# A fused attention and gated-MLP kernel on one core: an input load, a reduction and a bound are moved in the first passes

## The chip, the core and the metric

The kernel runs on one core of a Trainium2 chip. A core has five engines that run their own instruction streams beside each other and meet only at semaphores: TensorE (PE in the profile; PEld is its weight load), VectorE (DVE), ScalarE (ACT), GpSimd (POOL) and SyncE (SP, which here only issues DMAs). The metric is device time of one execution in microseconds (us); lower is better. The kernel before took 1939.83 us, the median of three runs (1937.18, 1939.83 and 1940.55).

## The reference, cut to what matters

```
xn = layernorm(x)                                   # x: 2048 x 640
q  = xn @ wq                                        # 32 heads of 192
p  = softmax(q @ k_cache.T * 192**-0.5)             # 2048 queries x 2048 keys, per head
s  = (p @ v_cache) @ wo
g  = silu((silu(xn @ w1) * (xn @ w3)) @ w2)         # F = 1536
out = x + s * g
```

All tensors are bf16. Softmax doesn't need the exact maximum of a row: any shift that is no smaller than the scores, and not so large that the sums vanish, gives the same result.

## The kernel before, in words

**Tiling.** The 2048 queries are 16 tiles of 128 rows (x tiles 0 to 15), taken in four blocks of 512 (`qb` 0 to 3). A head's pass over one block has eight steps `p` 0 to 7. In a step TensorE makes the scores of two key tiles for the 512 queries (`scores`, six 64-row matmuls on line 505 into one of two PSUM tiles `st2`), ScalarE takes the exponential (`weights`, line 512, with the shift `nb` as bias) and TensorE multiplies by the values (`values`, line 545, 16 matmuls, into the two PSUM tiles `ob0` and `ob1`). At the end of a pass `evict` (line 521) reduces each of the two on VectorE; the next pass can't write `ob0` or `ob1` before its reduction is done. `values` returns pieces that are put in a list, and `advance` takes them from it some steps late, so that TensorE has work while ScalarE makes the exponentials.

**The bound.** The shift `nb` isn't the row maximum but an upper bound of the block: for each of the 192 dimensions the largest absolute query times the largest absolute key, summed. `query_max` (line 376) and `key_maxima` (line 414) make the maxima on VectorE and keep them in the tile `st`; `bound` (lines 442 to 448) multiplies them, sums two columns into `ns`, and lets GpSimd sum over the 128 partitions (`partition_all_reduce`, line 448). For the first two heads only part of the data is looked at, and `compare_bounds` later computes the full bound and keeps the difference in `gaps`; if that were over 32, or a sum vanished, an exact path would be run. `next_bound(h, qb)` is the bound of head `h` for one block.

**The first passes.** They go in the order of `order`: (head 0, block 0), (head 1, block 0), (0, 1), (0, 2), (0, 3), (1, 1), (1, 2), (1, 3). So the pass of head 1 over block 0 is the second and the pass of head 0 over block 1 is the third. Into these passes the layer norm of the x tiles is woven by hand: `extras` and `posts` name what follows step `p` of pass `n`, as `(n, p)`. A tile's layer norm is `ln_stats` (two `bn_stats` and a `bn_aggr` on VectorE, lines 237 and 238), `ln_root` (logarithm and exponential on ScalarE, lines 244 and 247), `ln_scale` (VectorE, line 255) and `dma_turn` (a transposing DMA issued by SyncE, line 266, into `xnT`). Around the change:

- `(0, 0)`: `complete_second`, GpSimd's copies of head 1's keys into `KC` (lines 154 and 155, columns 0 to 511 and then 512 to 1023 of a half) and a memset of ones
- `(0, 2)`: scale and turn x tiles 4 and 5, and the first key maxima of head 1
- `(0, 4)`: `next_bound(1, 0)`, the shift of the second pass
- `(0, 5)`: `ln_stats` of x tiles 6 and 7
- `(1, 0)`, `(1, 1)`: `ln_root(6)`; scale and turn tiles 6 and 7
- `(1, 5)`: `ln_root(8, 4)` and `late_project(0, 1)`, head 0's queries of block 1 (line 348). Its first part has ten matmuls on x tiles 4 and 5 and then ten on 6 and 7; the casts, the maxima, `next_bound(0, 1)` and a copy of rows into `qD` (`lower_rows`, line 388) follow in `second`.

In the passes `n` = 3 to 6 a list `looked[h]` of further maxima is worked off on VectorE, one or two per step; it ends with `compare_bounds(h)`.

**The order of the transfers.** Nearly all loads of the start are on SyncE's queue, in program order: keys of head 1 (`KB`, line 124), the first part of head 1's values (`load_values_part`, line 143, two DMAs), then x tiles 6 and 7 (`load_x`, line 194), x tiles 8 and 9, the second part of head 1's values, x tiles 10 and 11; then the transposes of x tiles 4 to 7. `pin` keeps the program order of an engine for what it wraps; everything that the change touches is pinned.

After the first passes come the heads 2 to 31 (a whole head takes about 51 us), the rest of the MLP, and the output projection.

Of the kernel before, what the change touches and what calls it, by code (L numbers as in the profile page):

```python
# [30 lines left out]
def _kernel_impl(ctx, tc, A_x, A_k_cache, A_v_cache, A_wq, A_wo, B_w1, B_w3, B_w2, out):  # L31
    nc = tc.nc
# [33 lines left out]
    pin = tc.keep_in_program_order  # L66
# [35 lines left out]
    def load_weights(h, eng, keep):  # L102
        w = wqp.tile([P, DC, 2 * P], BF16, tag="w")
        wsel = B_w1 if h % 2 == 0 else B_w3
        m = h // 2

        def load(c0, c1, src, s0):
            return lambda eng: keep(eng.dma_start(out=w[:, :, c0:c1],  # L108
                                                  in_=src[:, s0:s0 + c1 - c0].rearrange("(c p) d -> p c d", p=P)))

        if h < 2:
            steps = [load(0, DH, A_wq, h * DH), load(DH, 2 * P, wsel, m * PGW)]
        else:
            steps = [load(0, P, A_wq, h * DH), load(P, P + PGW, wsel, m * PGW), load(P + PGW, 2 * P, A_wq, h * DH + P)]
        ws = (w[:, :, 0:P], w[:, :, P:2 * P])
        if eng is None:
            return ws, steps
        for step in steps:
            step(eng)
        return ws  # L120

    def load_key_part(h, s, half, k0, k1, keep):
        d0 = (0, DH - P)[s]
        return keep(nc.sync.dma_start_transpose(out=half[:, k0:k1], in_=A_k_cache[0, h][k0:k1, d0:d0 + P]))  # L124

    def load_key_half(h, s, keep):
        half = kvp.tile([P, SK], BF16, tag=("KA", "KB")[s], name=("KA", "KB")[s])
        load_key_part(h, s, half, 0, SK, keep)
        return half
# [9 lines left out]
    def load_values_part(h, vt, r0, r1):  # L139
        of = A_v_cache[0, h].rearrange("(t r p) d -> p t r d", t=2, p=P)  # L140
        to = vt[:].rearrange("p (t r) d -> p t r d", t=2)
        for t in range(2):
            pin(nc.sync.dma_start(out=to[:, t, r0:r1, 0:DH], in_=of[:, t, r0:r1, :]))  # L143

    def complete_head(h, ws, ks, vt, keep, parts=1):
        (wq, wqB), (KA, KB) = ws, ks
        KC = kvp.tile([P, HALF], BF16, tag="KC")
        loads[h] = dict(KA=KA, KB=KB, KC=KC, vt=vt, wq=wq, wqB=wqB)

        def ones():  # L150
            keep(nc.gpsimd.memset(vt[:, :, DH:DH + 1], 1.0))

        def copies(c0, c1):
            turn = [lambda: keep(nc.gpsimd.tensor_copy(out=KC[ROWS[1], c0:c1], in_=KA[ROWS[0], HALF + c0:HALF + c1])),
                    lambda: keep(nc.gpsimd.tensor_copy(out=KC[ROWS[0], c0:c1], in_=KB[ROWS[1], c0:c1]))]
            return [step() for step in (turn[::-1] if h == 1 else turn)]

        if parts > 1:
            ones()
            return [lambda c0=c0: copies(c0, c0 + HALF // parts) for c0 in range(0, HALF, HALF // parts)]  # L160
        return lambda: (ones(), copies(0, HALF))
# [13 lines left out]
    loads = {}  # L175

    with ExitStack() as actx:
# [15 lines left out]
        def load_x(eng, t0, t1):  # L193
            pin(eng.dma_start(out=x_all[:, t0:t1, :], in_=x2[t0 * P:t1 * P, :].rearrange("(t p) d -> p t d", p=P)))

        first_st = [new_st(nc.gpsimd) for _ in range(2)]
        first_ws, first_loads = zip(*(load_weights(h, None, pin) for h in range(2)))
# [95 lines left out]
        KA1 = load_key_half(1, 0, pin)  # L293
        load_values_part(0, values0, 4, 8)
        keys1 = KA1, load_key_half(1, 1, pin)
        values1 = kvp.tile([P, NKT, DH + 2], BF16, tag="vt", name="vt")
        load_values_part(1, values1, 0, 4)
        load_x(nc.sync, 6, 8)
        load_x(nc.sync, 8, 10)
        load_values_part(1, values1, 4, 8)  # L300
        load_x(nc.sync, 10, 12)
# [71 lines left out]
        def query_max(h, qb, s, n=512):  # L373
            hd = heads[h]
            src, r = ((hd["qA"], slice(0, P)), (hd["qF"], ROWS[not hd["up"]]))[s]
            pin(nc.vector.tensor_reduce(out=hd["st"][r, 2 + s, qb:qb + 1], in_=src[r, qb * 512:qb * 512 + n],  # L376
                                        axis=AX.X, op=ALU.max, apply_absolute_value=True))

        def swap_rows(h, qb, copy=nc.gpsimd.tensor_copy):
            hd, qs = heads[h], slice(qb * 512, (qb + 1) * 512)  # L380
            keep = pin if h < 2 else (lambda x: x)
            return [lambda t=t: keep(copy(out=hd["qS"][ROWS[t], qs], in_=hd["qA"][ROWS[1 - t], qs]))  # L382
                    for t in range(2)]

        def lower_rows(h, qb, copy=nc.gpsimd.tensor_copy):
            hd, qs = heads[h], slice(qb * 512, (qb + 1) * 512)
            keep = pin if h < 2 else (lambda x: x)
            keep(copy(out=hd["qD"][ROWS[hd["up"]], qs], in_=hd["qF"][ROWS[1 - hd["up"]], qs]))

        def project_casts(h, qb, ps, cast):  # L390
            hd, qs = heads[h], slice(qb * 512, (qb + 1) * 512)
            pin(nc.scalar.copy(out=hd["qA"][:, qs], in_=ps[:, 0:512]))  # L392
            pin(cast(out=hd["qF"][:, qs], in_=ps[:, 512:1024]))  # L393
            upper, lower = swap_rows(h, qb)
            upper()
            if (h, qb) == (0, 1):
                lower()
            elif hd["up"]:
                lower_rows(h, qb)
                lower()  # L400
            else:
                lower()
                lower_rows(h, qb)

            def maxima():
                query_max(h, qb, 0)
                query_max(h, qb, 1)

            return maxima

# [218 lines left out]
        query_max(1, 0, 1)  # L629

        def complete_second():
            for step in complete_head(1, first_ws[1], keys1, values1, pin, 2):
                step()
            heads[1].update(L=loads.pop(1), vt=values1)

        def late_project(h, qb):
# [30 lines left out]

        all_keys = [(s, cb) for cb in range(NQB) for s in range(2)]
        looked = {h: [(key_maxima, h, s, cb) for cb in range(NQB) for s in range(2) if cb or s] for h in range(2)}
        looked[0] += [(query_max, 0, 0, s) for s in range(2)]  # L670
        for h in range(2):
            looked[h] += [(other_low_maxima, h), (compare_bounds, h)]
        key_slots = list(all_keys)
# [12 lines left out]
        }  # L686
        posts = {
            (0, 0): ((complete_second,),),
            (0, 2): ((ln_root, 4), (scale_and_turn, 4), (scale_and_turn, 5), (first_key_maxima, 1)),
            (0, 4): ((next_bound, 1, 0),),  # L690
            (0, 5): ((ln_stats, 6), (ln_stats, 7)),
            (1, 0): ((ln_root, 6),),
            (1, 1): ((scale_and_turn, 6), (scale_and_turn, 7), (load_x, nc.sync, 12, 16)),
# [344 lines left out]
@with_exitstack  # L1038
def kernel(
    ctx: ExitStack,  # L1040
    tc: tile.TileContext,
    A_x: bass.AP,
    A_k_cache: bass.AP,
    A_v_cache: bass.AP,
    A_wq: bass.AP,
    A_wo: bass.AP,
    B_x: bass.AP,
    B_w1: bass.AP,
    B_w3: bass.AP,
    B_w2: bass.AP,  # L1050
    out: bass.AP,
):
    _kernel_impl(ctx, tc, A_x, A_k_cache, A_v_cache, A_wq, A_wo, B_w1, B_w3, B_w2, out)
# [30 lines left out]
```

## Time and profile before

| what | us |
|---|---|
| runs: lowest, median, highest | 1937.18, 1939.83, 1940.55 |
| the profiled execution's own time | 1938.53 |
| its span, first to last instruction | 1936.7 |
| outside the span (1938.53 - 1936.7) | 1.83 |
| TensorE busy in the span | 1929.3 |
| TensorE waits for VectorE's `osum`: total, longest | 2.0, 1.6 |

The page is one execution, taken by the hardware profiler. A line of a timeline reads: start in us, duration in us, engine, line of the kernel and operation, what it writes `<-` what it reads, how many instructions were merged, and in brackets how long the engine stood idle before it and what ended that. SPq is SyncE's queue issuing a DMA. A line of the stretches ("windows") gives, for each engine, the busy time in that stretch (and the number of instructions), then the granted TensorE clock as a share of full speed, the DMA engines' busy share, and GB/s.

### The profile page before, as it was taken

The page shows a single profiled execution, that of the slowest core. Times are in us where ns is not written, and L with a number is a line of the kernel's source. Part 1 is how long each engine was busy: PE and PEld are TensorE (multiplying, and loading weights), DVE is VectorE, ACT ScalarE, POOL GpSimd, SP SyncE. Part 2 cuts the span into 40 slices and gives each one's busy share as a digit, 9 for nine tenths or more (in the row PEclk, how much of TensorE's full clock was granted, in tenths as well). Part 3 has the DMA queues.
Part 4 walks back from the last instruction along what each step waited for, and adds up shares of the span by engine and source line. Part 5 has one row for each costly group of instructions (what it writes and reads, how often), then busy time and mean ns, then how long its engine had stood idle before and what let it go on. Part 6 is the DMA issues. An engine that isn't in the chain of part 4 may idle for free.

```text
span 1936.7 us, 60453 instructions
## 1 busy us (share of the span) xinstructions
PE 1929.3 (100%) x27269; PEld 1418.6 (73%) x27269; DVE 1030.3 (53%) x1890; ACT 1278.1 (66%) x1296; POOL 414.4 (21%) x637
## 2 busy tenths in 40 slices
PE   9999999999999999999999999999999999999999
PEld 6779999999777766666666666666666666577776
DVE  6775556565656555556555565555565654421111
ACT  6777777777777777777777777777777777210000
POOL 1432222222222222222222222222221110000000
PEclk9999999999999999999999999999999999999999
DMA  8532423231212233233433232323232102937883
GB/s 179 107 76 49 82 47 85 47 74 38 69 46 71 55 64 65 63 82 77 109 55 77 55 76 55 76 47 85 47 84 38 41 10 75 277 67 138 157 150 59
DMA packets 361672, 152.84 MB, mean 79 GB/s; under 512 B 312544, under 2 KB 355232, under 8 KB 361408
## 3 DMA queue, kind: packets, MB, share of 16 engines
q1 hardware_dynamic: 346832, 120.12, 29.6%
q0 software_dynamic: 7872, 23.60, 4.7%
q10 hardware_dynamic: 6704, 5.21, 1.1%
q8 instruction: 214, 3.51, 0.8%
q14 instruction: 50, 0.41, 0.1%
HBM read 56.23 MB, written 31.98 MB: 46 GB/s over the span
## 4 chain that ended last, share of the span: by engine, by line
PE 98%; DVE 1%; SPq 1%; DMA 0%; issue 0%; ACT 0%
PE st L505 34%; PE obank L545 34%; PE ps L348 14%; PE ps_s L864 11%; PE ps_f L888 3%; PE ps_gu L332 1%; PE ps_gu L348 0%; SPq L124 0%; DMA x_all<-in_A_x_dram 0%; DVE osum L521 0%; DVE st L237 0%; SPq L143 0%; DVE st L414 0%; DVE pa L486 0%; DVE ostage L528 0%; DVE qF L393 0%
## 5 line engine op out<-in xcount | busy, mean ns | idle before, releaser
L512 ACT ACTIVATE pT<-st,nb 128x1024 bf16<-128x1024 f32 x960 | 1068.4, 1113 | 326.6 <-PE st L505 322.2
L545 PEld LDWEIGHTS <-pT 64*128 64x128 bf16 x16384 | 758.3, 94 | 200.7 <-issue 4.1
L545 PE MATMUL obank<-vt,pT 64*128 64x193 bf16 x16384 | 875.4, 243 | 2.1 <-DVE osum L521 2.0
L521 DVE TENSOR_REDUCE osum<-obank 128x386 f32<-128x772 f32 x256 | 234.3, 956 | 579.8 <-PE obank L545 579.8
L505 PE MATMUL st<-qA,KA 64*128 64x512 bf16 x2048 | 411.7, 376 | 0.1
L505 PE MATMUL st<-qS,KC 64*128 64x512 bf16 x1024 | 385.2, 376 | 0.0
L505 PE MATMUL st<-qS,KB 64*128 64x512 bf16 x1024 | 385.1, 376 | 0.0
L505 PE MATMUL st<-qF,KB 64*128 64x512 bf16 x960 | 361.0, 376 | 0.0
L505 PE MATMUL st<-qD,KC 64*128 64x512 bf16 x960 | 361.0, 376 | 0.0
L348 PE MATMUL ps<-xnT,w 64*128 64x512 bf16 (+1 forms) x2540 | 319.0, 374 | 0.0
L382 POOL COPY qS<-qA 64x512 bf16<-64x512 bf16 x254 | 160.4, 632 | 619.8 <-ACT qA L392 612.8
L505 PEld LDWEIGHTS <-KC 64*128 64x128 bf16 x2048 | 192.2, 94 | 98.5 <-issue 0.2
L348 PEld LDWEIGHTS <-w 64*128 64x128 bf16 x2540 | 148.3, 94 | 95.4
L864 PE MATMUL ps_s<-wo_sb,oT 128*128 128x320 bf16 (+2 forms) x1536 | 208.8, 299 | 0.0
L505 PEld LDWEIGHTS <-KB 64*128 64x128 bf16 x2048 | 192.3, 94 | 5.6
L864 PEld LDWEIGHTS <-oT 128*128 128x128 bf16 x1536 | 148.4, 98 | 60.4
L528 DVE TENSOR_TENSOR ostage<-osum,rl_all 128x384 bf16<-128x384 f32 x256 | 155.1, 606 | 8.8
L505 PEld LDWEIGHTS <-KA 64*128 64x128 bf16 x2048 | 128.8, 93 | 15.6 <-issue 1.6
L108 POOL DMA_DIRECT2D w<-in_A_wq_dram x60 | 52.9, 882 | 289.1 <-PE ps L348 288.9
L393 DVE CAST qF<-ps 128x512 bf16<-128x512 f32 x120 | 82.9, 691 | 52.0 <-ACT qA L392 51.8
L869 DVE SCALAR_TENSOR_TENSOR tmp<-ps_s,g_all 128x320 f32<-128x320 f32 (+2 forms) x32 | 15.6, 488 | 176.0 <-PE ps_s L864 176.0
L376 DVE TENSOR_REDUCE st<-qA 128x1 f32<-128x512 bf16 (+1 forms) x129 | 87.0, 674 | 4.2 <-ACT qA L392 4.0
(101 smaller groups left out, 1135.1 us busy)
## 6 DMA issues: line engine op xcount, KB each, us to landing
o_scr<-ostage SPq DMA_DIRECT2D x64, 384.0 KB, 2.8
vt<-in_A_v_cache_dram SPq DMA_DIRECT2D x30, 768.0 KB, 6.2
wo_sb<-in_A_wo_dram POOLq DMA_DIRECT2D x1, 7680.0 KB, 32.6
w<-in_A_wq_dram POOLq DMA_DIRECT2D x30, 160.0 KB, 3.5
hT_scr<-hblk SPq DMA_DIRECT2D x16, 256.0 KB, 3.0
xt<-in_A_x_dram POOLq DMA_DIRECT2D x16, 160.0 KB, 8.9
w<-in_B_w_dram POOLq DMA_DIRECT2D x30, 80.0 KB, 2.6
w<-in_A_wq_dram POOLq DMA_DIRECT2D x30, 80.0 KB, 2.8
```

The costliest lines, as they stand in the source:

```text
L108: return lambda eng: keep(eng.dma_start(out=w[:, :, c0:c1], in_=src[:, s0:s0 + c1 - c0].rearrange("(c p) d -> p c d", p=P)))
L348: mm = pin(nc.tensor.matmul(out[:, t * 512 + t0 * P:t * 512 + (t0 + step) * P], lhsT=ws[t][ROWS[r], c, :], rhs=rows_of(qb, c, ROWS[r], t0, ...
L376: pin(nc.vector.tensor_reduce(out=hd["st"][r, 2 + s, qb:qb + 1], in_=src[r, qb * 512:qb * 512 + n], axis=AX.X, op=ALU.max, apply_absolute_ ...
L382: return [lambda t=t: keep(copy(out=hd["qS"][ROWS[t], qs], in_=hd["qA"][ROWS[1 - t], qs])) for t in range(2)]
L393: pin(cast(out=hd["qF"][:, qs], in_=ps[:, 512:1024]))
L505: pin(nc.tensor.matmul(st2[:, t * 512:(t + 1) * 512], lhsT=keys, rhs=q[ROWS[t], qs], start=(s == 0), stop=(s == 2)))
L512: pin(nc.scalar.activation(out=pT2[:, c0:c1], in_=st2[:, c0:c1], func=ACT.Exp, scale=SCALE, bias=nb))
L521: pin(nc.vector.tensor_reduce(out=osum[:], in_=ob[:].rearrange("p t (j c) -> p j c t", j=2)[:, :, 0:DH + 1, :], axis=AX.X, op=ALU.add))
L528: pin(nc.vector.tensor_tensor(out=ostage[:, b * 2:b * 2 + 2, hg * DH:(hg + 1) * DH], in0=osum[:, :, 0:DH], in1=rl.unsqueeze(2).to_broadcas ...
L545: pin(nc.tensor.matmul(acc["o"][b][:, r, j * 256:j * 256 + DH + 1], lhsT=pT2[ROWS[r], t * 512 + i * P:t * 512 + (i + 1) * P], rhs=vt[ROWS[ ...
L864: pin(nc.tensor.matmul(ps, lhsT=oT[:, k, :], rhs=wo_sb[:, k, c0:c1], start=(k == 0), stop=(k == OC - 1)))
L888: pin(nc.tensor.matmul(ps[:, pi * 512:pi * 512 + c1 - c0], lhsT=hT[:, fc, qsl], rhs=w2_sb[:, fc, c0:c1], start=(fc == 0), stop=(fc == FC - ...
```

## The change

Three edits:

- On SyncE's queue the load of x tiles 6 and 7 is issued ahead of the first part of head 1's values, and no longer behind it.
- `complete_second` does only the first half of head 1's key copies. The second half is kept in `loads["second half"]` and run behind `next_bound(1, 0)`, and both are put at `(0, 3)`. On GpSimd the sum over the partitions so stands ahead of the last two key copies. VectorE's order in the second pass is as before.
- For head 0, block 1, `query_max` looks at 256 of the 512 queries. The full maxima of that block are made later, in `looked[0]`, which gets two items more (VectorE).

```
@@ the loads of the start
         keys1 = KA1, load_key_half(1, 1, pin)
+        load_x(nc.sync, 6, 8)
         values1 = kvp.tile([P, NKT, DH + 2], BF16, tag="vt", name="vt")
         load_values_part(1, values1, 0, 4)
-        load_x(nc.sync, 6, 8)
         load_x(nc.sync, 8, 10)
@@ project_casts
             def maxima():
-                query_max(h, qb, 0)
-                query_max(h, qb, 1)
+                n = 256 if (h, qb) == (0, 1) else 512
+                query_max(h, qb, 0, n)
+                query_max(h, qb, 1, n)
@@ complete_second
         def complete_second():
-            for step in complete_head(1, first_ws[1], keys1, values1, pin, 2):
-                step()
+            first, loads["second half"] = complete_head(1, first_ws[1], keys1, values1, pin, 2)
+            first()
             heads[1].update(L=loads.pop(1), vt=values1)
@@ first passes
-        looked[0] += [(query_max, 0, 0, s) for s in range(2)]
+        looked[0] += [(query_max, 0, qb, s) for qb in range(2) for s in range(2)]
...
-            (0, 4): ((next_bound, 1, 0),),
+            (0, 3): ((next_bound, 1, 0), (lambda: loads.pop("second half")(),)),
```

No other instruction is added, and TensorE's order is the same.

## The prediction

> **What bounds the kernel now.** I read the chain of work that ended last, by engine, and then the list of waits.
>
> ```profile
> PE 98%; DVE 1%; SPq 1%; DMA 0%; issue 0%; ACT 0%
> ```
>
> ```profile
> PE obank L545 <- DVE osum L521: 2.0, 2, 1.6
> ```
>
> TensorE carries 98% of the span, so an edit elsewhere pays only where TensorE stands still. Behind the preamble its only listed waits are two on the `osum` reductions, 2.0 us. TensorE's timeline has them in one place:
>
> ```profile
> 24.44 0.38 PE L505 MATMUL st<-qA,KA 64*128 64x512 bf16 x2
> ...
> 28.11 0.51 PE L545 MATMUL obank<-vt,pT 64*128 64x193 bf16 x8 [1.65 <-DVE osum L521]
> 28.98 1.44 PE L545 MATMUL obank<-vt,pT 64*128 64x193 bf16 x16 [0.36 <-DVE osum L521]
> ...
> 32.63 0.40 PE L505 MATMUL st<-qA,KA 64*128 64x512 bf16 x2
> ```
>
> The pace when nothing stops it stands in the chain in order of time, a little later: six score matmuls in 0.65 us, 16 value matmuls in 0.67. The 16 at 28.98 took 1.44.
>
> ```profile
> 32.81 0.65 PE st L505 x6
> 33.46 0.67 PE obank L545 x16
> ```
>
> The stretches say why:
>
> ```profile
> 26.30:28.98 2.68, 0.68 (x10) 0.34 (x8) 2.65 (x6) 1.68 (x4) 0.00 (x0) 1.00 1.38 161
> 28.98:32.43 3.45, 3.45 (x34) 2.71 (x35) 3.37 (x10) 1.51 (x2) 0.00 (x0) 0.51 0.70 141
> ```
>
> In the first, TensorE (second column) is busy 0.68 of 2.68 us and VectorE (fourth) 2.65. In the second TensorE is busy throughout, with a granted clock of 0.51. So the stall is paid twice: 2.00 us of idling, and then 3.45 * (1 - 0.51) = 1.69 us of lost clock. What VectorE did meanwhile:
>
> ```profile
> 22.69 0.15 DVE L445 TENSOR_REDUCE ns<-pr 128x1 f32<-128x2 f32 x1
> 25.11 0.89 DVE L237 BATCH_NORM_STATS2 st<-x_all 128x6 f32<-128x320 bf16 x2 [2.26 <-DMA x_all<-in_A_x_dram]
> ```
>
> It idles 2.26 us, until x tiles 6 and 7 land at 25.1. Their statistics follow, and the two reductions of the ended pass are queued behind them; so TensorE gets `ob0` at 28.11 and `ob1` at 28.98.
>
> From 24.44 to 32.63 TensorE does three sets of scores and 48 value matmuls: 3 * (0.65 + 0.67) = 3.96 us of work in 8.19. So **4.23 us is the most that this place can give**.
>
> **The load, and the sum ahead of the copies.** SyncE's queue with the two issues that change places, GpSimd's keys and sum, ScalarE's wait for the shift, and the sizes by the DMA issues of the first 45 us (the last column is issue to landing):
>
> ```profile
> 19.42 1.13 SPq L143 DMA_DIRECT2D vt<-in_A_v_cache_dram  x2
> 20.59 1.02 SPq L194 DMA_DIRECT2D x_all<-in_A_x_dram  x2
> ```
>
> ```profile
> 21.38 0.61 POOL L155 COPY KC<-KB 64x512 bf16<-64x512 bf16 x1 [4.91 <-DMA KB<-in_A_k_cache_dram]
> ...
> 24.07 0.38 POOL L448 PARTITION_ALL_REDUCE nb_all<-ns  x1
> ```
>
> ```profile
> 24.48 1.11 ACT L512 ACTIVATE pT<-st,nb_all 128x1024 bf16<-128x1024 f32 x1 [0.81 <-POOL nb_all L448]
> ```
>
> ```profile
> vt<-in_A_v_cache_dram SPq DMA_DIRECT2D x8, 192.0 KB, 3.9
> x_all<-in_A_x_dram SPq DMA_DIRECT2D x4, 320.0 KB, 5.2
> ...
> xnT<-xn SPq DMA_TRANSPOSE x8, 2.6
> ```
>
> From the keys' landing (GpSimd's copy starts at 21.38) to that of x (25.1), 2 * 192 + 320 = 704 KB came in 3.7 us, 190 KB per us. With x first, only 320 KB lie between: 1.69 us, landing at **23.07**. The bounds are 21.38 (at once) and 25.1 (the order of issue doesn't matter). I take 23.07, which uses the rate of these very transfers. VectorE is free at 22.84 (22.69 + 0.15), so its statistics start 2.02 us earlier, and all behind them moves along.
>
> TensorE then runs so. The third set of scores needs a PSUM tile that the exponential at 24.48 empties; this one waited 0.81 us for the shift. GpSimd's sum now stands ahead of the last two key copies, may start when `ns` is there at 22.84, and ends near 23.4. So these scores start when the matmuls ahead of them are through: 24.44 + 0.65 + 0.33 (half of 16 values) = 25.42, to 26.07. `ob0` is free at 28.11 - 2.02 = 26.09, eight matmuls last to 26.42, `ob1` is free at 28.98 - 2.02 = 26.96: 0.54 us of idling are left. Then 16 values (27.63), scores (28.28), 16 values (28.95). Before, this point was 32.63: 3.68 us gained. I take full clock here, as 0.56 us idle is far under the 2.00 that went ahead of the drop.
>
> **What is late next.** The transposes of x tiles 4 to 7 on SyncE's queue, which `late_project(0, 1)` reads; and its 20 matmuls on TensorE, 1.09 us to the next line:
>
> ```profile
> 23.37 3.52 SPq L266 DMA_TRANSPOSE xnT<-xn  x1
> ...
> 26.99 1.22 SPq L266 DMA_TRANSPOSE xnT<-xn  x1
> ```
>
> ```profile
> 35.09 1.27 PE L348 MATMUL ps<-xnT,w 64*128 64x256 bf16 x20
> 36.18 0.40 PE L505 MATMUL st<-qA,KA 64*128 64x512 bf16 x2
> ```
>
> The first (tile 4) was on the queue for 3.52 us, three times the second's 1.22; I take this as a matter of the transfers ahead of it, whose sum is unchanged, and leave it. Tile 5 ends at 28.21. Tiles 6 and 7 are scaled earlier than that (the second reduction now ends near 26.9), so they issue back to back from 28.3 and 29.6 (a gap of 0.1 each, as from 26.89 to 26.99), and tile 7 lands 2.6 later, at 32.2. TensorE would reach its second ten matmuls, which read tiles 6 and 7, at 35.09 + 0.55 - 3.68 = 31.96. It waits about 0.25, and **3.43 us** of the gain is left. So an x landing before 23.3 brings nothing more, and each us after it costs one.
>
> **The third pass.** VectorE where head 0's second block begins, ahead of it a 256-column maximum of the first block, and the idle time ahead of a later reduction; then TensorE:
>
> ```profile
> 11.85 0.42 DVE L376 TENSOR_REDUCE st<-qA 128x1 f32<-128x256 bf16 x1
> ...
> 38.76 0.69 DVE L376 TENSOR_REDUCE st<-qA 128x1 f32<-128x512 bf16 x1 [0.80 <-ACT qA L392]
> 39.36 0.67 DVE L376 TENSOR_REDUCE st<-qF 64x1 f32<-64x512 bf16 x1
> ...
> 40.45 0.29 DVE L388 COPY qD<-qF 64x512 bf16<-64x512 bf16 x1
> ...
> 82.94 1.83 DVE L521 TENSOR_REDUCE osum<-obank 128x386 f32<-128x772 f32 x2 [4.58 <-PE obank L545]
> ```
>
> ```profile
> 40.50 0.38 PE L505 MATMUL st<-qF,KC 64*128 64x512 bf16 x1
> 40.79 0.37 PE L505 MATMUL st<-qD,KB 64*128 64x512 bf16 x1
> ```
>
> The matmul on `qD` starts 0.29 us after its partner on `qF`, because VectorE's copy ends at 40.74. The first maximum shrinks by 0.69 - 0.42 = 0.27, the second alike, so the copy ends near 40.2, before 40.50. Gain **0.25** (between 0 and 0.29). The full maxima are made up for later: 0.69 + 0.67 = 1.4 us at most in the passes before 82.94, where VectorE idles 4.58 us. Cost nothing; without that cover 1.4.
>
> **What costs nothing.** Head 1's first values are issued 0.55 us later (half of 1.13) and land behind 320 KB more. They are read at 26.09. Such DMAs landed 3.9 us after issue in the median; from a second issue at 20.55 that is 24.5, with the 5.2 of the x row 25.8. Cost 0; each tenth beyond 26.09 would first eat the wait to 26.96. SyncE's later issues keep their times. GpSimd's last two key copies, of 0.61 us each, move by about the sum's 0.38 and some waiting and end by 24.7; the scores that read them are those at 28.95.
>
> **The sum.** 3.43 + 0.25 = 3.7 us, against the profiled execution's 1938.53 (span 1936.7 and 1.83 around it): 1934.8. That execution lies 1.30 under the median of the three runs. The four together (1937.18, 1938.53, 1939.83, 1940.55) have their middle at 1939.18, which I take as the base: **1935.5 us**. A measurement of this kernel can tell about 0.2%, 3.9 us, from no change, so the bound for "faster" is 1939.83 - 3.88 = 1935.95, just above the forecast.
>
> **The rivals.**
>
> *The clock drop is not in every execution.* 1.69 of the us hang on it, and the executions shown differ by 3.4 us, which is room for such a thing. If the executions that set the median had the stall without the drop, `late_project` would come 1.69 earlier there; 3.7 - 1.7 = 2.0 are left: 1937.2. Against it: the one trace has the drop. [...] Chance 0.15.
>
> *The order of issue doesn't move the landing.* If the queue's transfers share the engines evenly, x lands at 25.1 as before. Then the statistics, the reductions and the drop stay, and only the third pass' 0.25 is gained: 1938.9. For it: several transfers are in flight at once. Against it: the DMA share (the last column but one of the stretches) is 1.38 there, so the engines are full and what is ahead takes its turn. Chance 0.05.
>
> *The transposes bind harder.* If the 3.52 us grow by one, tile 7 lands at 33.2 as before, and 1 us of the gain goes: 1936.5. Chance 0.07. **Slower** by the same mechanism: TensorE's second ten matmuls stood at 35.64. From a landing of tile 7 after 35.64 on, the place gives nothing; each us beyond costs one, and a wait over 2 us brings the clock drop with 1.69 back. SyncE would have to be held up 3.4 us more than I reckon (35.6 - 32.2) for no gain, and 5.5 or more for a loss: at 37.8 it is 2.2 + 1.7 - 0.25 = 3.7 us, 1942.9. The queue carries no more than before, which speaks against it. Chance 0.04, half of it beyond 1943.7.
>
> *The transposes bind less.* If tile 4's 3.52 us was a wait for the value transfers that now go later, tiles 5 to 7 could issue sooner, the cap falls and up to 4.23 + 0.25 = 4.5 us come: 1934.7. Chance 0.12.
>
> **How the numbers follow.** The forecast has the rest, 0.57, with times from 1934.6 to 1936.4. The range takes it, the better case and the clock rival: 1933.8 to 1938.0, leaving out about 0.15. Faster by over 0.2%: 0.12 of the better case and some 0.42 of the forecast's 0.57, 0.54. Slower by over 0.2%: 0.02 for the mechanism and 0.02 for what I don't see. The rest, 0.42, is the same.
>
> **What would show it.** In the profile after: the wait of the statistics on x at most 0.3 us in place of 2.26; the shift's sum starting near 23 in place of 24.07 and no `nb` wait on ScalarE there; the waits on `osum` under 0.7 us in place of 2.0; a granted clock of 1.00 from 26 to 36; the scores of 32.63 near 29; a gap of some 0.25 us within the first 20 projection matmuls, near 32; the `qD` matmul 0.02 behind its partner; the span near 1933.0. A clock below 1 anywhere from 26 to 45 us, or x landing after 24, would make it wrong.

## The result, and the profile after

The changed kernel took 1936.40 us, the median of 22 runs (1934.53 to 1940.46); the kernel before, in 22 runs beside them, 1939.14 us (1936.45 to 1941.41). The ratio is 0.9986 with a 95% interval of 0.998 to 0.9993: faster by 0.14%, which lies within the 0.2% that the prediction set as its bound for "the same" (it gave that 0.42, and 0.54 to a larger gain). The forecast was 1935.5 with a range of 1933.8 to 1938.0. The profiled execution took 1934.81 us with a span of 1933.0, where the prediction's sum gave 1934.8 and 1933.0. So the sum came out between the two profiled executions, and the median lies 0.9 us above its forecast. Most of this part is about that difference.

From TensorE's list of waits, after (us in total, times, longest):

```profile
PE obank L546 <- DVE osum L522: 0.4, 1, 0.4
```

The 2.0 us on `osum` are one wait of 0.36. (The change moves this code down by one line, so 545 is now 546.) The same place on TensorE's timeline:

```profile
24.63 0.38 PE L506 MATMUL st<-qA,KA 64*128 64x512 bf16 x2
...
26.32 0.51 PE L546 MATMUL obank<-vt,pT 64*128 64x193 bf16 x8
...
27.19 0.84 PE L546 MATMUL obank<-vt,pT 64*128 64x193 bf16 x16 [0.36 <-DVE osum L522]
...
29.17 0.40 PE L506 MATMUL st<-qA,KA 64*128 64x512 bf16 x2
```

From the second scores (24.63) to the fifth (29.17) it is 4.54 us in place of 8.19. The 16 value matmuls that took 1.44 at a granted clock of 0.51 take 0.84 at 1.00; the 0.36 us of waiting lie ahead of them. The stretches, with the granted clock as the third column from the end:

```profile
24.63:29.17 4.54, 4.18 (x70) 2.93 (x68) 4.47 (x12) 3.52 (x6) 0.52 (x1) 1.00 1.20 229
27.19:32.43 5.24, 5.24 (x94) 4.25 (x95) 4.53 (x14) 4.07 (x5) 0.00 (x0) 1.00 1.02 147
```

TensorE is busy 4.18 of the 4.54 us, then without a hole to 32.43, at full clock. VectorE, whose lateness was the cause, and SyncE's two exchanged issues:

```profile
23.10 0.15 DVE L446 TENSOR_REDUCE ns<-pr 128x1 f32<-128x2 f32 x1
23.32 0.89 DVE L237 BATCH_NORM_STATS2 st<-x_all 128x6 f32<-128x320 bf16 x2
...
25.36 1.78 DVE L522 TENSOR_REDUCE osum<-obank 128x386 f32<-128x772 f32 x2
```

```profile
19.78 0.58 SPq L194 DMA_DIRECT2D x_all<-in_A_x_dram  x1
20.40 1.02 SPq L143 DMA_DIRECT2D vt<-in_A_v_cache_dram  x2
```

The statistics follow the shift's product with no wait on x (it was 2.26 us), and the two reductions start at 25.36, just behind them. The x tiles had landed by 23.32; how long before, this trace can't say. In the two other profiles of the changed kernel VectorE waits 0.2 us for them, and they land at 22.93 and 24.09.

### The profile page after: what moved, and what is told of

The parts are those of the page before. It is cut to its first block, busy times and chain, and to the rows that moved or that the text cites. A ratio compares the mean times of both kernels' runs of the same rounds, so it can differ in the third digit from the quotient of the medians.

```text
span 1933.0 us, 60455 instructions
## 1 busy us (share of the span) xinstructions
PE 1926.7 (100%) x27269; PEld 1411.1 (73%) x27269; DVE 1029.6 (53%) x1892; ACT 1278.1 (66%) x1296; POOL 414.5 (21%) x637
## 4 chain that ended last, share of the span: by engine, by line
PE 98%; DVE 1%; SPq 1%; DMA 0%; issue 0%; ACT 0%
PE st L506 35%; PE obank L546 34%; PE ps L348 14%; PE ps_s L865 11%; PE ps_f L889 3%; PE ps_gu L332 1%; PE ps_gu L348 0%; SPq L124 0%; DMA x_all<-in_A_x_dram 0%; DVE osum L522 0%; DVE st L237 0%; SPq L143 0%; DVE st L415 0%; DVE pa L487 0%; DVE ostage L529 0%; DVE qF L393 0%
```

## The experiments

The theory under test is the prediction's: the early load ends VectorE's wait, TensorE's stall goes, and with it the clock drop. The rivals are that one of the other two edits brings a part, that the drop comes or goes for a reason other than the stall (as the "phase": where the stall lies against stretches, or windows, of the clock; when it was put up it was a supposition), and, for the missing 0.9 us, that something behind the place takes it back. Each ratio below is against the kernel before on the same chip, with its 95% interval.

### The kernel before, once more

Its edit is none; it gives the spread.

> The kernel before, unchanged, to see the granted clock of each of its executions. Theory A (the clock drop behind the stall comes in part of the executions only): the mean clock is 0.999 (one half-speed window of 3.4 us is 1.7 us, 0.09% of the span) in 40 to 80% of them and 1.000 in the others, and the executions with 1.000 lie about 1.7 us lower. Theory B (the drop comes every time, and the 1 us between the gain of the two profiled executions, 3.7, and of the medians, 2.7, is from elsewhere): 0.999 in all.

1940.1 us (11 runs, 1936.93 to 1942.75), ratio 1.000 [0.9991, 1.0009]. Each execution's mean granted clock is known too, and this orders them: seven had 0.999 (1939.53 to 1940.53), one 0.998 (1942.75) and three 1.000 (1936.93 to 1938.47). Of the 33 other runs of the kernel before in this group of experiments, 21 had 0.999, with a median of 1939.92, three had 0.998 (1941.19 to 1942.09), and 9 had 1.000, with a median of 1937.04. The drop is in some 7 of 10 executions, not in all.

### Edit 1 alone: the load

```
         keys1 = KA1, load_key_half(1, 1, pin)
+        load_x(nc.sync, 6, 8)
         values1 = kvp.tile(...)
         load_values_part(1, values1, 0, 4)
-        load_x(nc.sync, 6, 8)
```

> Only x tiles 6 and 7 ahead of the second head's values. Theory A (the late landing of x is the whole cost of the place): VectorE's wait on x under 0.3 us, the waits on osum together 0.3 to 0.8 us instead of 2.0, no clock drop in the profile, and the stretch from the second pass' second scores to its fifth 4.5 to 4.9 us instead of 8.19, though ScalarE still waits some 0.7 us for the shift; the time 2.2 to 3.5 us below before. Rival (the shift's sum is needed as well, because ScalarE's wait for it becomes the bound): the stretch stays over 5.2 us and the gain is under 1.5 us.

1937.16 us, ratio 0.9988 [0.9979, 0.9997]; 10 of 11 executions had no drop. VectorE's statistics of x tiles 6 and 7, the place and TensorE's one wait in it, then TensorE's longest wait and the one of ScalarE on the shift:

```profile
23.77 0.89 DVE L237 BATCH_NORM_STATS2 st<-x_all 128x6 f32<-128x320 bf16 x2
```

```profile
25.00:29.62 4.62, 4.23 (x71) 2.95 (x69) 4.38 (x11) 3.96 (x6) 0.33 (x1) 1.00 1.40 223
```

```profile
26.53 0.39 PE L505 MATMUL st<-qA,KA 64*128 64x512 bf16 x2 [0.39 <-ACT pT L512]
```

```profile
PE ps L348 <- DMA xnT<-xn: 1.7, 1, 1.7
```

```profile
ACT pT L512 <- POOL nb_all L448: 1.1, 1, 1.1
```

The statistics no longer wait for x. The place is 4.62 us long, about as with all three edits (4.54), though ScalarE still waits 1.1 us for the shift; that now shows as 0.39 us of TensorE's waiting, on ScalarE's exponential, where the changed kernel has 0.36 on `osum`. But a new wait is the longest: 1.7 us for the transposes that `late_project(0, 1)` reads. That is the prediction's "late next", at seven times its 0.25.

### Edit 2 alone: the sum ahead of the copies

```
+            first, loads["second half"] = complete_head(1, ...)
+            first()
...
-            (0, 4): ((next_bound, 1, 0),),
+            (0, 3): ((next_bound, 1, 0), (lambda: loads.pop("second half")(),)),
```

> Only the shift's sum ahead of the last two key copies. Theory A: the sum starts 0.6 to 1.1 us earlier and ScalarE's wait for it goes, but VectorE still waits 2.2 us for x, TensorE 2.0 us for osum; stretch 8.0 to 8.2 us, time within 0.4 us of before. Rival (the sum is part of the stall): 0.7 us or more gained.

1939.27 us, ratio 0.9996 [0.9987, 1.0005]: nothing to be measured. The place and its wait:

```profile
25.04:34.10 9.06, 5.85 (x71) 3.97 (x68) 6.96 (x18) 3.53 (x6) 0.67 (x2) 0.81 0.88 167
```

```profile
PE obank L545 <- DVE osum L521: 3.2, 1, 3.2
```

TensorE comes to the value matmuls earlier and waits longer there for the same reductions, behind the same x tiles: VectorE waited 3.2 us for x and TensorE 2.5 on `osum` in the kernel before, once more, and here 3.1 and 3.2. With the load in its old place the shift isn't what arrives last.

### Edit 3 alone: half of the queries

```
+                n = 256 if (h, qb) == (0, 1) else 512
+                query_max(h, qb, 0, n)
...
-        looked[0] += [(query_max, 0, 0, s) for s in range(2)]
+        looked[0] += [(query_max, 0, qb, s) for qb in range(2) for s in range(2)]
```

> Only the third pass' shift from half of the queries. Theory A: the stall and the clock drop stay as before; the matmul on qD starts 0 to 0.15 us behind its partner instead of 0.29; 0.1 to 0.3 us gained in the profile, nothing that the times can tell. Rival (the shift is late for ScalarE too): over 0.5 us.

1939.26 us, ratio 1.0001 [0.9992, 1.001]. In its profile VectorE's product and TensorE's pair of matmuls are:

```profile
40.58 0.45 DVE L443 SCALAR_TENSOR_TENSOR pr<-st 128x2 f32<-128x2 f32 x1
```

```profile
41.40 0.38 PE L506 MATMUL st<-qF,KC 64*128 64x512 bf16 x1
41.59 0.37 PE L506 MATMUL st<-qD,KB 64*128 64x512 bf16 x1
```

The `qD` matmul still starts 0.19 behind its partner, where it was 0.29 before. The product of two columns, which is queued ahead of the copy into `qD`, took 0.45 us.

### The changed kernel again, and the load half way

The first is the changed kernel as it is. The second starts from the kernel before and puts x tiles 6 and 7 between the two DMAs of the first values, with the other two edits left out:

```
-        load_values_part(1, values1, 0, 4)
+        load_values_part(1, values1, 0, 4, (0,))
         load_x(nc.sync, 6, 8)
+        load_values_part(1, values1, 0, 4, (1,))
```

> The changed kernel, unchanged, a second profile and the clock of each execution. Theory A (the stall gone, and its length decides the clock drop): at most 2 in 10 executions with mean clock 0.999, median 2.3 to 3.2 us below before. Theory C (in part of the executions the transposes of x tiles 6 and 7 are late, as the 1.72 us wait in the profile of the load alone): the profile may show a wait of TensorE on xnT of 0 to 2 us near 32.

> From the kernel before: x tiles 6 and 7 between the two DMAs of the values' first part, half of the move. Theory A: VectorE waits about 1.2 us on x, TensorE about 1 us on osum, the clock drop in 0 to 4 of 10 executions, time 1.2 to 2.5 us below before. Rival (phase alone): drop in 7 of 10, time 0.6 to 1.2 us below before.

The changed kernel: 1936.78 us, ratio 0.9983 [0.9974, 0.9992], no drop in 11 executions. The load half way: 1936.85 us, ratio 0.9984 [0.9975, 0.9993], no drop in 10 of 11. The place of the second:

```profile
25.04:30.27 5.23, 4.45 (x70) 2.96 (x68) 5.13 (x14) 4.07 (x6) 0.07 (x1) 1.00 1.18 235
```

The gain was larger than expected (3.15 us between the medians of 1940.0 and 1936.85). The place is 0.69 us longer than in the first profile of the changed kernel (4.54), and the median time is the same. No wait for the transposes is in this profile, so what half of the move leaves at the place, the full move may lose at the projection; one profile doesn't show it. The two intervals overlap almost wholly, so neither can be called faster.

### The load later

From the kernel before, the other way round: the second part of the values, too, goes ahead of x tiles 6 and 7.

```
         load_values_part(1, values1, 0, 4)
+        load_values_part(1, values1, 4, 8)
         load_x(nc.sync, 6, 8)
         load_x(nc.sync, 8, 10)
-        load_values_part(1, values1, 4, 8)
```

> From the kernel before: x tiles 6 and 7 also behind the second part of the values, 384 KB more ahead of them. Theory A: x lands about 2 us later than before, the waits on osum grow from 2.0-3.2 to 4-5 us, the clock drop is in 9 of 10 executions or more, time 1.5 to 3 us above before. Rival (the windows' phase alone decides the drop): drop in 7 of 10 as before.

1942.13 us, ratio 1.001 [1.0001, 1.0019]. All 11 executions had a drop, 8 of them a mean clock of 0.998. VectorE's wait on x, TensorE's on the reductions, and the place:

```profile
28.68 0.89 DVE L237 BATCH_NORM_STATS2 st<-x_all 128x6 f32<-128x320 bf16 x2 [4.38 <-DMA x_all<-in_A_x_dram]
```

```profile
31.68 2.35 PE L545 MATMUL obank<-vt,pT 64*128 64x193 bf16 x24 [3.76 <-DVE osum L521]
```

```profile
25.60:36.37 10.77, 6.62 (x71) 4.60 (x68) 7.52 (x20) 4.65 (x6) 0.29 (x1) 0.71 0.73 152
```

So the order of issue does move the landing, in both directions: the statistics that need x start at 28.68 here, at 25.11 in the prediction's profile and at 23.77 with the load first (the prediction's rival that it doesn't is out), and with this longer stall the drop came in all 11 executions.

### The kernel before in an execution without the drop

Two single profiles of the kernel before, to meet such an execution.

> Another profile of the kernel before, to catch an execution without the clock drop (3 in 10 have none). Theory A (the length of the stall decides): without a drop, the waits on osum are clearly under the 2.0 of the profiles with one, 1.5 us or less, since x landed sooner. Rival (the phase of the clock windows decides): without a drop the waits are 2.0 us or more, and a window edge lies within the stall. With a drop it tells nothing new: waits of 2.0 us or more.

> As the look before: without a drop, osum waits of 1.5 us or less by theory A, of 2.0 or more by the rival; with a drop, 2.0 or more.

They took 1937.08 and 1937.70 us, both at a clock of 1.000. The first:

```profile
PE obank L545 <- DVE osum L521: 2.0, 2, 1.6
```

```profile
24.68:31.18 6.50, 4.45 (x70) 2.96 (x68) 5.74 (x15) 4.07 (x6) 0.02 (x1) 1.00 1.12 193
```

The waits are those of the prediction's profile, 2.0 us in two, and the clock did not fall. The place is 6.50 us long and not 8.19: the difference is 1.69, exactly the price that the prediction gave to the drop. But a wait of 2.0 us had a drop in one profile and none in the other, so the theory that its length alone decides falls. The second profile has waits of 1.7 us and no drop, between what the two theories expected.

What differs is where the stall lies against a grid of 3.413 us. In the trace of the kernel before, the records of the granted clock start at 5.17, 29.06, 32.48 and 1937.11 us, which is 7, 1 and 558 times 3.413 us apart; in the trace of the changed kernel at 4.07 and 1932.60, 565 times 3.413 us apart. TensorE alone, in two of the grid's stretches of the kernel before (busy time, granted clock, DMA share, GB/s), then in two of the first of these profiles:

```profile
25.65:29.06 3.41, 1.41 (x16) 1.00 1.30 184
29.06:32.47 3.41, 3.41 (x35) 0.50 0.71 145
```

```profile
27.20:30.61 3.41, 1.92 (x33) 1.00 1.10 115
30.61:34.03 3.42, 3.42 (x66) 1.00 0.69 116
```

In the kernel before the stall lies in one stretch, which has 1.41 us of work, and the next is granted 0.50. In the second pair an edge of the grid, at 27.20, cuts the stall in two, so that its emptiest stretch still has 1.92 us, and the next is granted 1.00. The clock is 1.00 on both sides of that edge, so its place is an estimate, the grid carried on. Such stretches around the place were read in thirteen of the fourteen profiles. The five at full clock ahead of a drop had TensorE busy for 0.26, 0.82, 0.86, 1.16 and 1.41 us; those with 1.69 us or more (1.69, 1.71, 1.92 and above) had none behind them. None lies between 1.41 and 1.69, and a rule beyond these profiles isn't shown. At half clock, where the load is later, 1.82 us of work was followed by a second stretch at half clock. This is read from the profiles and wasn't set up as a test.

### The changed kernel in an execution above its first profile

> A third profile of the changed kernel. Theory A: osum waits under 0.7 us, no drop. Theory C (late transposes): a wait of TensorE on xnT of 0.3 to 2 us near 32 would show it; the two profiles so far have none.

1937.27 us at a clock of 1.000. The place is 4.72 us (4.54 in the first profile). The projection, whose second ten matmuls read tiles 6 and 7, in this third profile and then in the first profile after:

```profile
32.40 0.72 PE L348 MATMUL ps<-xnT,w 64*128 64x256 bf16 x10
34.52 0.72 PE L348 MATMUL ps<-xnT,w 64*128 64x256 bf16 x10 [1.40 <-DMA xnT<-xn]
```

```profile
31.63 1.27 PE L348 MATMUL ps<-xnT,w 64*128 64x256 bf16 x20
```

Here is missing time: 1.40 us between the two tens, and none in the first profile. The transpose of tile 7 on SyncE's queue, with its time from issue to landing, in the third profile and then in the first:

```profile
30.30 1.23 SPq L266 DMA_TRANSPOSE xnT<-xn  x1
...
xnT<-xn SPq DMA_TRANSPOSE x1, 4.2
```

```profile
29.44 1.23 SPq L266 DMA_TRANSPOSE xnT<-xn  x1
...
xnT<-xn SPq DMA_TRANSPOSE x1, 2.7
```

The queue took it up 0.9 us later than in the first profile, and from there the landing took 1.5 us longer. What the DMA engines moved from 31.5 to 34.5 us, in 40 slices of 0.075 (GB/s), and the instruction queue's row in the half microsecond in which it has one (packets, MB, share of the engines): the third profile, 31.5 to 32, and then the first, 33.5 to 34.

```profile
GB/s 44 355 174 205 212 191 205 181 198 133 34 3 0 0 0 0 0 0 7 10 7 7 10 10 7 14 10 7 14 195 172 0 102 137 188 154 85 85 17 51
...
q8 instruction: 1, 0.02, 15.9%
```

```profile
GB/s 45 0 0 0 0 0 85 85 171 119 85 119 51 51 85 68 68 85 119 188 273 358 307 324 290 341 341 393 375 375 427 560 410 324 427 324 410 273 307 222
...
q8 instruction: 1, 0.02, 11.7%
```

In the third profile 0 to 14 GB/s move from 32.4 to 33.6, and the transpose ends only after that. In the first its last bytes have moved by 31.6, it lands at 32.1, and what follows reaches 220 to 560 GB/s from 33 on. In the third profile a transfer of the instruction queue (q8, 0.02 MB) starts between 31.5 and 32, while tile 7's transpose is under way; in the first it starts at 33.5 to 34, when that transpose has landed, and falls into the next one, which takes 3.7 us and for which TensorE doesn't wait. The three profiles in which TensorE waits over 1 us for tile 7 (this one 1.4 us, edit 1 alone 1.7, the copy first 1.5) have the transfer at 31.5 to 32, 31.5 to 32 and 32 to 32.5; the two of the changed kernel without a wait at 33.5 to 34 and 34 to 34.5, and the load half way, also without, at 35 to 35.5. It shows in the kernel before, too: its transposes issued at 36.91, 38.22 and 39.53 landed 2.6 us after their issue and the one at 40.85 after 4.1, with such a transfer starting at 42.0. In these profiles the two go together; that the one causes the other wasn't tried, and the experiment that follows has a late transpose without such a transfer.

### The transposes ahead of the later loads

From the changed kernel, to take that wait away: x tiles 8 to 11 and the second part of the values are issued behind the transposes of tiles 4 and 5.

```
-        load_x(nc.sync, 8, 10)
-        load_values_part(1, values1, 4, 8)
-        load_x(nc.sync, 10, 12)
...
-            (0, 2): (..., (scale_and_turn, 5), (first_key_maxima, 1)),
+            (0, 2): (..., (scale_and_turn, 5), (load_x, nc.sync, 8, 10),
+                     (load_values_part, 1, values1, 4, 8), (load_x, nc.sync, 10, 12), (first_key_maxima, 1)),
```

> From the changed kernel: x tiles 8 and 9, the second part of the values, and x tiles 10 and 11 are issued behind the transposes of tiles 4 and 5 and no longer ahead of them. Theory C (the transposes are what limits the changed kernel, held up by the transfers ahead of them on the queue): tile 4's transpose is on the queue under 2 us, no wait on xnT, the executions draw together, median 0.3 to 1.0 us below the changed kernel of the same chip. Rival (the transposes were not what limits; the later x tiles 8 to 11 hold up their statistics): same time or up to 1 us more, with a wait of VectorE on x tiles 8 to 11.

1936.50 us, ratio 0.9987 [0.9978, 0.9996], no better than the changed kernel beside it (1936.78, 0.9983). SyncE's first two transposes here and in the kernel after, then the wait for transposes (line 345 is line 348 of the others) and VectorE at the next x tiles, both here:

```profile
22.35 2.58 SPq L266 DMA_TRANSPOSE xnT<-xn  x2
```

```profile
23.72 4.31 SPq L266 DMA_TRANSPOSE xnT<-xn  x2
```

```profile
PEld L345 <- DMA xnT<-xn: 0.3, 1, 0.3
```

```profile
30.10 0.89 DVE L237 BATCH_NORM_STATS2 st<-x_all 128x6 f32<-128x320 bf16 x2 [1.04 <-DMA x_all<-in_A_x_dram]
```

The first two transposes hold the queue for 2.58 us in place of 4.31, and the wait for transposes is 0.3 us in this profile, on a weight load. But x tiles 8 and 9 are now late, VectorE idles 1.04 us for them, and two of the 11 executions have the drop. And the transpose of tile 7 still lands late, 3.5 us after its issue at 30.04, with no transfer of the instruction queue within it (it starts at 35 to 35.5), but with the moved loads. So that transfer isn't the only thing that goes with a late landing. The expected gain didn't come: the queue's delay went and another lateness came in.

### The copy ahead of the bound

From the changed kernel, for the third pass: in `second` of `late_project` the copy into `qD` goes ahead of `next_bound(0, 1)`.

```
                 rest()()
-                if h < 2:
-                    next_bound(h, qb)
                 if (h, qb) == (0, 1):
                     lower_rows(h, qb, nc.vector.tensor_copy)
+                if h < 2:
+                    next_bound(h, qb)
```

> From the changed kernel: VectorE's copy into qD ahead of the product pr and the sum ns of the third pass' shift. In the changed kernel's profiles pr takes 0.38 to 0.39 us in place of 0.16 and ends as GpSimd's two copies into qS end. Theory D (VectorE is held while GpSimd copies): the qD copy, issued about 0.4 us ahead of GpSimd's end, takes 0.5 to 0.75 us in place of 0.29 and ends about 0.3 us behind GpSimd's end, pr takes 0.16, and the matmul on qD follows its partner by 0.02 us. Rival (pr is slow for another reason, its data): the copy takes 0.29 us, pr 0.39 again. No difference that the time can tell, under 0.15 us.

A single execution, 1937.23 us at a clock of 1.000, with 1.5 us of the transposes' wait; one time can't tell a difference this small. Its product, its copy, GpSimd's copies beside them, and TensorE's pair; then the same of the kernel after:

```profile
38.76 0.52 DVE L388 COPY qD<-qF 64x512 bf16<-64x512 bf16 x1
39.32 0.16 DVE L443 SCALAR_TENSOR_TENSOR pr<-st 128x2 f32<-128x2 f32 x1
```

```profile
37.86 1.28 POOL L382 COPY qS<-qA 64x512 bf16<-64x512 bf16 x2 [12.03 <-ACT qA L392]
```

```profile
39.59 0.38 PE L506 MATMUL st<-qF,KC 64*128 64x512 bf16 x1
39.59 0.38 PE L506 MATMUL st<-qD,KB 64*128 64x512 bf16 x1
```

```profile
36.23 0.39 DVE L443 SCALAR_TENSOR_TENSOR pr<-st 128x2 f32<-128x2 f32 x1
...
36.84 0.29 DVE L388 COPY qD<-qF 64x512 bf16<-64x512 bf16 x1
```

```profile
35.33 1.28 POOL L382 COPY qS<-qA 64x512 bf16<-64x512 bf16 x2 [10.17 <-ACT qA L392]
```

After, the product runs from 36.23 to 36.62, and GpSimd's copies end at 35.33 + 1.28 = 36.61. With the copy first, the product starts behind the end of GpSimd's copies (37.86 + 1.28 = 39.14) and takes 0.16; the copy takes 0.52, from 38.76 to 39.28, and ends 0.14 behind them (0.3 was expected). Whichever of the two runs beside GpSimd is the slow one. Here the `qD` matmul starts with its partner, and the stretch from the third pass' first scores to its fourth is 4.18 us in place of 4.30.

## Why the prediction was right, and what it mis-sized

**The bound, the stall and its double price: right.** Edit 1 alone takes away the x wait, all but 0.39 us of the stall and, in 10 of 11 executions, the drop. The load half way and the load later show the same step at two other lengths of the stall. The drop's 1.69 us came out as 8.19 - 6.50 = 1.69. (The prediction's 1.44 beside 0.67 compares two views: a timeline gives 16 value matmuls 0.83 at full clock. Its 1.69 is worked out from the granted clock and doesn't need that.)

**The place: right to a few hundredths.** Predicted 28.95 - 24.44 = 4.51 us, measured 4.54, 4.18 and 4.72 in the changed kernel's three profiles. Of the predicted 0.54 us of waiting, 0.36, none and 0.36 were left. The clock there is 1.00 in all three, as the prediction asked; but two of the 22 timed executions (1936.10 and 1940.46) have a mean clock of 0.999, so a drop somewhere. In the third profile x landed at 24.09, past the 24 that the prediction named as a sign of being wrong; that execution's place began 0.58 us late as a whole, and it came out even so. The matmuls of the second half of the keys and the values' first DMAs, priced at nothing, delayed nothing.

**The sum ahead of the copies: not needed.** The prediction counted it as a condition of the new order, but edit 1 alone has a place of 4.62 us while ScalarE waits 1.1 us for the shift. That lies within the changed kernel's own 4.18 to 4.72, so no worth of this edit can be read from the place, and by itself it brought nothing.

**The transposes, "a wait of about 0.25": the step that failed.** The term is "tile 7 lands 2.6 later", which gave one landing time, 32.2, and a wait of 0.25. The two profiles of the changed kernel that took 1934.81 and 1934.65 have no wait: tile 7 landed 2.7 and 2.6 us after its issue, at 32.1 and 31.6, and TensorE came to its second ten matmuls no earlier than that. The execution that took 1937.27 has a wait of 1.40: there it landed 4.2 us after its issue, at 34.5. So the term has at least two values. The other part, "I take this as a matter of the transfers ahead of it, whose sum is unchanged, and leave it", did little harm: tile 4 was on the queue for 2.5 to 3.1 us (3.52 before). The rival "the transposes bind harder", 1936.5 with a chance of 0.07, has the size of the loss but not its cause, since it let the 3.52 grow.

The changed kernel's 22 executions fall into groups: eight at 1934.53 to 1935.74, with a middle of 1935.1, twelve without a drop at 1936.33 to 1937.40, with a middle of 1937.0, and the two with a drop. The three profiles lie in these groups as their waits would have it; that the landing of a transpose sorts all of them isn't shown. Of the 2.46 us between the third profile (1937.27) and the first (1934.81), 1.59 lie at the projection (3.83 us from the scores ahead of it to those behind it, in place of 2.24), 0.18 in the place and 0.58 in the first pass. There VectorE waited 0.70 us for x tiles 4 and 5, in place of 0.20, ScalarE's logarithm of the layer norm then waited 0.59 for VectorE, and the place began at 25.21 in place of 24.63.

**The clock drop not in every execution: true of the kernel before, but not of its median.** With a chance of 0.15 it was a rival, for the case that the median's executions have no drop; some 3 of 10 executions of the kernel before have none, and the median's has one. The 2.9 us between the medians with and without the drop (1939.92 and 1937.04) are more than 1.69. Three later profiles with a drop (the kernel before, edit 2 alone, edit 3 alone) also had longer waits on x, 2.8 to 3.2 us, where the prediction's profile had 2.26 and the two without a drop 2.0 and 2.2; so the two go together, and the rest is open.

**The third pass, "0.25": mis-sized, 0.15 of it came.** From the first to the fourth scores of the third pass it was 4.45 us before and 4.30 after. The `qD` matmul, asked for 0.02 behind its partner, is 0.13 behind:

```profile
37.04 0.38 PE L506 MATMUL st<-qF,KC 64*128 64x512 bf16 x1
37.17 0.37 PE L506 MATMUL st<-qD,KB 64*128 64x512 bf16 x1
```

The maxima shrank as reckoned, but the product on VectorE then started early enough to lie beside GpSimd's copies and took 0.39 us where it takes 0.16 (the kernel before, and the copy first). The prediction took VectorE's order alone and left out what runs beside it. The rows of the product fit a wait for GpSimd: it ends at 36.62, GpSimd's copies at 36.61. The copy into `qD` fits less well: with all of its 0.29 us behind GpSimd's end at 39.14 it would have ended at 39.43, and it ended at 39.28. What the two engines contend for isn't shown.

**The maxima made up for later cost nothing: right.** VectorE's idle time ahead of the reduction is still there, 3.39 us of the 4.58:

```profile
79.33 0.96 DVE L522 TENSOR_REDUCE osum<-obank 128x386 f32<-128x772 f32 x1 [3.39 <-PE obank L546]
```

**The sum: right between the two profiles, in part by luck.** 3.43 + 0.25 was forecast, and 1938.53 - 1934.81 = 3.72 measured between the two profiled executions. The place gave 3.65 and the third pass 0.15; the place began 0.19 later than before (24.63 and 24.44). The 0.25 that wasn't lost at the transposes makes up for the 0.10 that the third pass didn't bring and for most of that later start. It is luck, too, that the changed kernel's profiled execution was one of the better group. Between the medians the gain is 2.74. The base was right (1939.18 forecast, 1939.14 measured), so the missing 0.9 us is the changed kernel's: 1935.5 was the time of its better group, not of its middle.

**What stays open:** why the transposes land late in part of the executions. No version here is measurably faster than the changed kernel.

## What to carry to other kernels

When a stall goes, look at the next transfer that is due behind it and give it a spread, not one landing time: one profile shows one execution, and a wait that was hidden by the old stall may come in others (none and 1.40 us in two profiles here). TensorE's stall here cost nearly its own length a second time in lost clock (1.69 us for 2.00), in some executions and not in others. In these profiles the drop came behind stretches of 3.41 us at full clock with 1.41 us of work or less, and behind none with 1.69 or more; so price such a drop as a spread, too, and try to shorten the stall by a part (with the load half way 10 of 11 executions had no drop). Before a small VectorE instruction is moved earlier, see what GpSimd runs at the new time (a product took 0.39 us beside its copies in place of 0.16).

## What the runs showed of the hardware that was not expected

- In the kernel before, a stretch of 3.41 us at full clock in which TensorE was busy 1.41 us was followed by one at 0.50; in edit 1 alone one with 1.69 us was not followed by a drop. So the same 2.0 us of waiting cost 1.69 us of clock in one execution and nothing in another, in which the grid carried on has an edge within the stall.
- The transposing DMA of x tile 7, in the same order on the queue, landed 2.6 to 2.7 us after its issue in some executions and 3.5 to 4.4 us in others. In one late case the engines moved 0 to 14 GB/s for 1.2 us in the middle of it, after 0.02 MB of the instruction queue had started.
- A VectorE product of two columns took 0.38 to 0.45 us beside GpSimd's copies and 0.16 behind their end (the copy first); a copy of 64 rows of 512 took 0.52 and 0.29.
